# Scores over 128 rows filled up with zeros, a mask moved from VectorE to GpSimd, and a new order, in a gated mix of linear attention and softmax attention

## The chip, the cores and the metric

The kernel runs on one core of a Trainium2 chip. The metric is the device time of one execution in microseconds (us), the median of several runs; lower is better.

## The reference

The input x has 2048 rows of 1024 columns. Two attention blocks read it, each with 32 heads of 32 columns, and a gate mixes their outputs. All data is 32-bit.

```
g = sigmoid((x * gate_w).sum(-1))
# block A: linear attention
q, k, v = split(x @ A_wqkv);  phi(t) = where(t > 0, t + 1, exp(t)) + 1e-6
kv  = phi(k).T @ v            # per head, 32 x 32
z   = phi(k).sum(over rows)   # per head
a   = (phi(q) @ kv) / (phi(q) . z + 1e-6) @ A_wo
# block B: softmax attention
b   = softmax(q @ k.T * 32 ** -0.5) @ v @ B_wo      # per head, q, k, v of x @ B_wqkv
out = g * a + (1 - g) * b
```

## The kernel before

Products that need more precision than one pass gives are made of three: each operand is split into a high and a low part, and `three` (L150 to L152) accumulates high x high, high x low and low x high in one PSUM bank, each pass 128 rows by 512 columns.

The work runs in stages. First half of V of block B, then all of Q and K (parts kept in DRAM as `qk_d`), on TensorE alone. Then four streams are interleaved by a planner. `maxima` makes scores of one head and takes the row maxima on VectorE (L695, L700); it runs one head and 12 passes (`LEAD`) ahead of the next stream. `heads_` makes the same scores transposed, one head later, with the negative maxima added by the product itself, and ScalarE takes the exponential (L831, L835); a pair of passes is one of each, 64 for every head. After every four tiles of 128 keys the products P V follow as a block of 32 matmuls on 32 columns each (L922), and the sums of P are kept by GpSimd (L877, L881, three quarters) and VectorE (L890). `linear` is the linear block in units of one row tile and one chunk of columns, 24 passes each: the second half of V ("v"), keys and values ("kv", four chunks), queries ("q", two chunks) and output ("o", two chunks). `output` is the last projection.

A head's scores need three products as well, of 32 rows each; they are stacked into one: `load_head` (L665 to L675) puts high, high, low parts of Q and high, low, high parts of K into rows 0 to 95 of two big tiles. Three pairs of such tiles rotate, a head's parts being loaded two heads ahead on SP's queue. Rows 96 and 97 of K hold ones, written by GpSimd when a tile is first used, and rows 96 and 97 of Q the high and low part of the negative maxima, which two DMAs bring (L720) once the head's maxima are done. So the maxima's scores go over 96 rows (L695) and the transposed scores over 98 (L831).

For the keys, `keys` (from L492) sums v phi(k) of four heads at a time in a 128 x 128 block of `kvb`; only the 32 x 32 blocks on its diagonal belong to a head. When a chunk's last row tile is in, two VectorE products with `heads` (ones on those blocks, zeros elsewhere) clear the rest (L509). The blocks are next read by `split_w` for the output's weights (L456).

The order on each engine is written out by hand in advance: the planner keeps a modelled time for every engine, from costs in microseconds (`MM` a matmul, `AV` and `AV_SWITCH` a block of P V products and the change to it), and lets the stream go on whose start is due and which lags most behind its rate. The linear stream's rate is counted in passes per pair: `RATE_Q` while queries run (a unit counts as 26 there, with its transposes), and for keys and output what then remains.

Of the kernel before, what the change touches and what calls it, by code (L numbers as in the profile page):

```python
# [18 lines left out]
P = 128  # L19
DH = 32  # L20
C = 512
# [5 lines left out]
AV_STEP = 4  # L27
WO_SLOT = 4
RESERVE = 56.0
RATE_Q = 1.75  # L30
AHEAD = {"head": 0, "max": 6, "lin": 6, "out": 0}
MM = 0.232
AV, AV_SWITCH = 0.88, 0.3
LATENCY = {"pe": 0.225, "act": 0.39, "dve": 0.36, "pool": 0.2}
SLACK = 0.4
WARM = 8
# [7 lines left out]
def kernel(  # L44
# [19 lines left out]
    nc = tc.nc  # L64
# [12 lines left out]
    def f32(ap):  # L77
        return ap.bitcast(F32)
# [24 lines left out]
    heads = sb.tile([P, P], F32, name="heads")  # L103
# [3 lines left out]
    kvb = sb.tile([P, NK, P], F32, name="kvb")  # L107
# [15 lines left out]
    bank = [psum.tile([P, C], F32, name=f"bank{i}") for i in range(8)]  # L123
# [34 lines left out]
    def use(eng, cost, *after):  # L158

        T[eng] = max(T[eng], *after, 0.0) + cost  # L160
        return T[eng] + LATENCY[eng]
# [9 lines left out]
    def defer(fn, at, cost=0.6, rank=1, prev=None):  # L171
        item = Later(fn, at, cost, rank, prev)
        later.append(item)
        return item
# [16 lines left out]
    def need(items):  # L191

        for item in items:
            if item.end is None:
                run(item)

    def ended(items, *also):

        if any(item.end is None for item in items):
            return None  # L200
        return max([0.0, *also] + [item.end for item in items])

    def fill(until):

        while True:
            fit = [it for it in later if due(it) and max(T["dve"], it.at) + it.cost <= until]
            if not fit:
                return
            run(min(fit, key=lambda it: (it.at > T["dve"] + 0.1, it.rank)))
# [6 lines left out]
    def bank_at():  # L216

        times = [ended(readers[b], free[b]) for b in RING if not held[b]]
        return min((at for at in times if at is not None), default=None)

    def take():

        idle = [b for b in RING if not held[b]]
        times = {b: ended(readers[b], free[b]) for b in idle}
        b = min(idle, key=lambda b: (times[b] is None, times[b] or 0.0))
        need(readers[b])
        free[b] = ended(readers[b], free[b])
        readers[b].clear()
        held[b] = True
        return b  # L230

    def give(b, at=0.0, items=()):

        held[b] = False
        free[b] = max(free[b], at)
        readers[b].extend(items)

    def both(*times):

        return None if None in times else max(times)  # L240
# [192 lines left out]
    def lin_pe(cost, *after):  # L433
        lin_done[0] += cost
        return use("pe", cost * MM, *after)

# [53 lines left out]
    def keys(c, t, pk, va, todo):  # L490

        yield lambda: both(ended(todo), bank_at())  # L492
        need(todo)
        b = take()
        pb = bank[b]
        end = lin_pe(2.0, free[b])
        for g in range(HC // P):
            nc.tensor.matmul(pb[:, g * P:(g + 1) * P], va[:, g * P:(g + 1) * P], pk[:, g * P:(g + 1) * P],  # L498
                             start=True, stop=True)
        acc = kvb[:, c * (HC // P):(c + 1) * (HC // P), :].rearrange("p k c -> p (k c)")  # L500

        def total(_):
            if t == 0:
                nc.vector.tensor_copy(acc, pb[:, :HC])
            else:
                nc.vector.tensor_add(acc, pb[:, :HC], acc)
            if t == NT - 1:
                for g in range(c * (HC // P), (c + 1) * (HC // P)):
                    nc.vector.tensor_mul(kvb[:, g, :], kvb[:, g, :], heads)  # L509

        item = defer(total, end, 0.34 if t < NT - 1 else 1.0, 1, k_left[-1] if k_left else None)
        give(b, 0.0, [item])
        k_left.append(item)
# [142 lines left out]

    stack_ready = [None] * H
    rows_ready = [None] * H  # L660
    s_done, st_done = [0], [0]
# [3 lines left out]
    def load_head(h):  # L665
        g, r = divmod(h, 4)
        rows = slice(r * DH, (r + 1) * DH)
        q, k = stack[h % 3]
        if h < 3:
            nc.gpsimd.memset(f32(k[3 * DH:3 * DH + 2, :]), 1.0)  # L670
        for b, (qp, kp) in enumerate(((0, 0), (0, 1), (1, 0))):
            nc.sync.dma_start(f32(q[b * DH:(b + 1) * DH, :]), qk_d[0][qp][g][rows, :])
            nc.sync.dma_start(f32(k[b * DH:(b + 1) * DH, :]), qk_d[1][kp][g][rows, :])
        stack_ready[h] = T["pe"] + 10.0
# [8 lines left out]
    def maxima():  # L683

        for h in range(H):
            yield lambda: stack_ready[h]
            q, k = stack[h % 3]
            m = mx[h % 2]
            for i in range(NT * NJ):
                t, j = divmod(i, NJ)  # L690
                if i:
                    yield bank_at
                b = take()
                end = use("pe", MM, free[b])
                nc.tensor.matmul(bank[b], q[:3 * DH, t * P:(t + 1) * P], k[:3 * DH, j * C:(j + 1) * C],  # L695
                                 start=True, stop=True)
                s_done[0] += 1
                fill(end + LATE)
                give(b, use("dve", 0.605, end))
                nc.vector.tensor_reduce(m[:, t, j:j + 1], bank[b], AX.X, ALU.max)  # L700
            rows(h, q, mneg[h % 2])
# [103 lines left out]
    def heads_():  # L805
        pr_t.extend(big_tile(6 + i, F32) for i in range(NPR))
        lacc_t.extend(big_tile(i, F32) for i in LACC)
        spare = big_tile(SPARE, F32)
        raws[2:6] = [spare[:, i * C:(i + 1) * C] for i in range(4)]
        o_ring.append(spare)  # L810
        o_ring.extend(pr_t[((H - 1) * NT + t) % NPR] for t in (NT - 6, NT - 4, NT - 3, NT - 2, NT - 1))
        tail = None
        for h in range(H):
            q, k = stack[h % 3]
            last = h == H - 1
            av_, sums = attend(h, lacc_t[h % 2])
            for t in range(NT):
                i = (h * NT + t) % NPR
                for j in range(NJ):
                    if j:  # L820
                        yield bank_at
                    elif t:
                        yield lambda: both(ended(pr_left[i], pr_free[i]), bank_at())
                    else:
                        yield lambda: both(ended(pr_left[i], pr_free[i]), bank_at(), rows_ready[h])
                    if j == 0:
                        need(pr_left[i])
                        pr_left[i].clear()
                    b = take()
                    end = use("pe", MM, free[b], rows_ready[h])  # L830
                    nc.tensor.matmul(bank[b], k[:3 * DH + 2, t * P:(t + 1) * P],  # L831
                                     q[:3 * DH + 2, j * C:(j + 1) * C], start=True, stop=True)
                    end = use("act", 0.49, end, pr_free[i])
                    give(b, end)
                    nc.scalar.activation(pr_t[i][:, j * C:(j + 1) * C], bank[b], AF.Exp, scale=SCALE)  # L835
                    st_done[0] += 1
                    if j == 1 and t and t % AV_STEP == 0:
                        yield from av_(t - AV_STEP)
                    elif j == 1 and tail:
                        yield from tail(NT - AV_STEP)  # L840
                        tail = None
                    if j == 2 and t == 0 and h + 2 < H:
                        load_head(h + 2)
                        load_v(h + 2)
                pr_end[i] = end
                sums(t)
                if last and t >= WO_SLOT:
                    wo_load()
                    if t >= WO_SLOT + 2:
                        wo_split()  # L850
                    else:
                        wo_load()
            tail = av_
        yield from tail(NT - AV_STEP)
        for items in pr_left:
            need(items)
        over["head"] = True
        load_all()
# [115 lines left out]
    def out_pe(n, c, k):  # L974
# [5 lines left out]
        for _ in three(bank[b], stat, [wo_part(k, p)[:, sl] for p in range(2)], k):  # L980
            use("pe", MM, free[b])

# [57 lines left out]
    steps = H * NT * NJ  # L1040
    rates = {"q": RATE_Q, "v": 0.0}
    rates["kv"] = rates["o"] = (cost["kv"] + cost["o"] - RESERVE) / (steps - cost["q"] / RATE_Q)
    goal = [warm]
# [107 lines left out]
```

## Time and profile before

| | before |
|---|---|
| median of 3 runs | 2994.87 us (2991.62 to 2995.91) |
| the profiled execution | 2999.18 us |
| its span, first to last instruction | 2997.4 us |
| mean granted TensorE clock | 0.997 |
| busy: TensorE, VectorE, GpSimd, ScalarE | 99%, 70%, 57%, 51% |

The profile is of one execution. PE is TensorE's matmuls, PEld its weight loads, DVE is VectorE, ACT ScalarE, POOL GpSimd and SP the engine that issues the DMAs. L695 is line 695 of the kernel. A matmul's length on the timeline is longer than the distance to the next one's start, since matmuls are pipelined: what one costs in a dense run is the distance of starts. Shapes such as 96*128 are rows by columns of the weights.

### The profile page before, as it was taken

Reading aid. Unit: us, or ns where it says so; the run is one execution under the profiler, and the core shown is the slowest. Engines: PE = TensorE matmul, PEld = TensorE weight load, DVE = VectorE, ACT = ScalarE, POOL = GpSimd, SP = SyncE. Lnnn points to the kernel's source line nnn. Section 1 sums busy time; section 2 is a strip of 40 time slices with the busy share of each in tenths; the row PEclk is TensorE's granted clock in tenths of the full one; section 3 lists DMA queues with packets and bytes.
Section 4 is the critical chain, followed back from the end, with each engine's and each line's share of the span. In section 5 each row is a group of like instructions: output and inputs, shape, how many; then the busy total and the mean of one; then the engine's idle time right before and its main releaser. Section 6 shows DMA issues by size and latency. Waiting matters only on the chain.

```text
span 2997.4 us, 41699 instructions
## 1 busy us (share of the span) xinstructions
PE 2975.5 (99%) x15072; PEld 2105.9 (70%) x15072; DVE 2109.7 (70%) x3464; ACT 1527.6 (51%) x2840; POOL 1721.8 (57%) x578
## 2 busy tenths in 40 slices
PE   9999999999999999999999999999999999999999
PEld 8888888766666666666666666666665666666687
DVE  3222115878888888878888889999998888886322
ACT  4111110566666656656666666666665655656200
POOL 0000000578887879878978886786676777773000
PEclk9999999999999999999999999999999999999999
DMA  6787333433434333333333344454442543424542
GB/s 192 216 265 224 120 114 92 124 85 89 117 88 99 90 98 99 96 82 110 95 85 85 108 119 118 121 152 128 117 122 100 126 117 100 112 84 142 204 158 70
DMA packets 259871, 364.51 MB, mean 122 GB/s; under 512 B 86480, under 2 KB 163280, under 8 KB 253520
## 3 DMA queue, kind: packets, MB, share of 16 engines
q1 hardware_dynamic: 259664, 361.84, 41.6%
q8 instruction: 119, 1.95, 0.3%
q14 instruction: 88, 0.72, 0.1%
HBM read 260.57 MB, written 100.66 MB: 121 GB/s over the span
## 4 chain that ended last, share of the span: by engine, by line
PE 93%; DVE 5%; DMA 1%; ACT 1%; issue 0%; SPq 0%; POOL 0%; ACTq 0%; DVEq 0%
PE bank L831 16%; PE bank L150 15%; PE bank L152 15%; PE bank L695 15%; PE bank L151 15%; PE bank L922 14%; DVE mx L700 2%; PE bank L498 1%; PE bank L739 1%; DVE bank L746 1%; DVE bank L890 0%; PE bank L456 0%; DMA big<-oA 0%; DVE kvb L509 0%; PE bank L535 0%
## 5 line engine op out<-in xcount | busy, mean ns | idle before, releaser
L881 POOL TENSOR_TENSOR big<-big,big 128x1536 f32<-128x1536 f32 x434 | 1516.3, 3494 | 305.5 <-ACT big L835 285.3
L700 DVE TENSOR_REDUCE mx<-bank 128x1 f32<-128x512 f32 x2048 | 1319.7, 682 | 321.1 <-PE bank L695 313.9
L835 ACT ACTIVATE big<-bank 128x512 f32<-128x512 f32 x2048 | 1184.1, 599 | 683.7 <-PE bank L831 639.0
L695 PE MATMUL bank<-big,big 96*128 96x512 f32 x2048 | 830.1, 406 | 5.1 <-DVE mx L700 2.1
L831 PE MATMUL bank<-big,big 98*128 98x512 f32 x2048 | 826.9, 404 | 2.6 <-DVE mx L700 2.4
L150 PE MATMUL bank<-big,big 128*128 128x512 f32 x2048 | 807.7, 394 | 6.8 <-DMA big<-oA 3.6
L152 PE MATMUL bank<-big,big 128*128 128x512 f32 x2048 | 805.6, 393 | 1.2 <-DMA big<-oA 0.8
L151 PE MATMUL bank<-big,big 128*128 128x512 f32 x2048 | 805.6, 393 | 0.0
L831 PEld LDWEIGHTS bank<-big,big 98*128 98x128 f32 x2048 | 389.6, 190 | 182.4 <-issue 80.2
L695 PEld LDWEIGHTS bank<-big,big 96*128 96x128 f32 x2048 | 388.0, 189 | 121.3 <-issue 14.7
L922 PE MATMUL bank<-big,mid 128*32 128x512 f32 x4096 | 465.2, 594 | 0.0
L150 PEld LDWEIGHTS bank<-big,big 128*128 128x128 f32 x2048 | 387.9, 189 | 95.4 <-DMA big<-oA 4.0
L152 PEld LDWEIGHTS bank<-big,big 128*128 128x128 f32 x2048 | 388.0, 189 | 85.9 <-DMA big<-oA 1.7
L151 PEld LDWEIGHTS bank<-big,big 128*128 128x128 f32 x2048 | 388.0, 189 | 83.1 <-issue 0.8
L922 PEld LDWEIGHTS bank<-big,mid 128*32 128x32 f32 x4096 | 123.1, 110 | 284.7 <-issue 284.7
L670 POOL MEMSET big<- 2x2048 f32 x3 | 5.4, 1806 | 544.4 <-PE bank L151 463.0
L890 DVE TENSOR_TENSOR bank<-bank,big 128x512 f32<-128x512 f32 x434 | 300.0, 691 | 14.4 <-ACT big L835 11.7
L257 DVE TENSOR_TENSOR mid<-bank,mid 128x512 fp32r<-128x512 f32 x64 | 44.3, 692 | 264.6 <-ACT mid L256 264.6
L256 ACT CAST mid<-bank 128x512 fp32r<-128x512 f32 x64 | 37.6, 587 | 291.6 <-PE bank L152 277.0
L877 POOL TENSOR_TENSOR big<-big,big 128x1536 f32<-128x1536 f32 x31 | 108.6, 3502 | 133.9 <-ACT big L835 128.1
L746 DVE RECIPROCAL bank<-bank 128x128 f32<-128x128 f32 x128 | 123.5, 965 | 5.8 <-PE bank L739 2.6
L257 DVE TENSOR_TENSOR big<-mid,big 128x512 fp32r<-128x512 f32 x96 | 64.1, 687 | 71.0 <-ACT big L256 70.9
(75 smaller groups left out, 1055.8 us busy)
## 6 DMA issues: line engine op xcount, KB each, us to landing
big<-xs SPq DMA_DIRECT2D x192, 512.0 KB, 4.1
big<-qk SPq DMA_DIRECT2D x192, 256.0 KB, 6.5
qk<-mid SPq DMA_DIRECT2D x128, 256.0 KB, 2.8
big<-oA SPq DMA_DIRECT2D x64, 512.0 KB, 4.8
xs<-big SPq DMA_DIRECT2D x64, 256.0 KB, 4.2
oA<-mid SPq DMA_DIRECT2D x64, 256.0 KB, 2.3
mid<-in_b_wqkv SPq DMA_DIRECT2D x48, 256.0 KB, 3.8
mid<-in_xT SPq DMA_DIRECT2D x32, 256.0 KB, 4.1
```

Source lines behind the costliest of these rows:

```text
L150: yield nc.tensor.matmul(ps, sh, mh_, start=(kt == 0), stop=False)
L151: yield nc.tensor.matmul(ps, sh, ml_, start=False, stop=False)
L152: yield nc.tensor.matmul(ps, sl, mh_, start=False, stop=(kt == NK - 1))
L695: nc.tensor.matmul(bank[b], q[:3 * DH, t * P:(t + 1) * P], k[:3 * DH, j * C:(j + 1) * C], start=True, stop=True)
L700: nc.vector.tensor_reduce(m[:, t, j:j + 1], bank[b], AX.X, ALU.max)
L746: nc.vector.reciprocal(pl[:, sl], pl[:, sl])
L831: nc.tensor.matmul(bank[b], k[:3 * DH + 2, t * P:(t + 1) * P], q[:3 * DH + 2, j * C:(j + 1) * C], start=True, stop=True)
L835: nc.scalar.activation(pr_t[i][:, j * C:(j + 1) * C], bank[b], AF.Exp, scale=SCALE)
L877: nc.gpsimd.tensor_add(lacc[:, :QP], pr(0)[:, :QP], pr(1)[:, :QP])
L881: nc.gpsimd.tensor_add(lacc[:, :QP], lacc[:, :QP], pr(t)[:, :QP])
L890: nc.vector.tensor_add(lacc[:, QP:] if t == NT - 1 else l_b[:, :n], l_b[:, :n], src)
L922: nc.tensor.matmul(av_b[j * DH:(j + 1) * DH, :], v[:, t, :], pr(t)[:, j * C:(j + 1) * C], start=(t == 0), stop=(t == NT - 1))
```

## The change

Scores' products, both ways round, go over all 128 rows. GpSimd fills rows 96 to 127 of both tiles with zeros at a tile's first use (the ones in K's rows 96 and 97 come after that). From the fourth head on, when a tile of Q is used again, a DMA copies two rows of zeros (98 and 99) over rows 96 and 97, in which the maxima of an earlier head stand. The mask on `kvb` goes from VectorE to GpSimd. Four planner constants change: `RATE_Q`, `MM`, `AV`, `AV_SWITCH`.

```diff
-RATE_Q = 1.75
+RATE_Q = 2.0
-MM = 0.232
-AV, AV_SWITCH = 0.88, 0.3
+MM = 0.2275
+AV, AV_SWITCH = 0.865, 0.35
...
             if t == NT - 1:
                 for g in range(c * (HC // P), (c + 1) * (HC // P)):
-                    nc.vector.tensor_mul(kvb[:, g, :], kvb[:, g, :], heads)
+                    nc.gpsimd.tensor_mul(kvb[:, g, :], kvb[:, g, :], heads)
...
         q, k = stack[h % 3]
         if h < 3:
+            for part in (q, k):
+                nc.gpsimd.memset(f32(part[3 * DH:, :]), 0.0)
             nc.gpsimd.memset(f32(k[3 * DH:3 * DH + 2, :]), 1.0)
+        else:
+            nc.sync.dma_start(f32(q[3 * DH:3 * DH + 2, :]), f32(q[3 * DH + 2:3 * DH + 4, :]))
...
-                nc.tensor.matmul(bank[b], q[:3 * DH, t * P:(t + 1) * P], k[:3 * DH, j * C:(j + 1) * C],
+                nc.tensor.matmul(bank[b], q[:, t * P:(t + 1) * P], k[:, j * C:(j + 1) * C],
                                  start=True, stop=True)
...
-                    nc.tensor.matmul(bank[b], k[:3 * DH + 2, t * P:(t + 1) * P],
-                                     q[:3 * DH + 2, j * C:(j + 1) * C], start=True, stop=True)
+                    nc.tensor.matmul(bank[b], k[:, t * P:(t + 1) * P], q[:, j * C:(j + 1) * C],
+                                     start=True, stop=True)
```

## Rows read from the trace of the kernel before

**Rows 1.** Page, part 1: busy us of each engine (share of the span), instructions.

```profile
PE 2975.5 (99%) x15072; PEld 2105.9 (70%) x15072; DVE 2109.7 (70%) x3464; ACT 1527.6 (51%) x2840; POOL 1721.8 (57%) x578
```

**Rows 2.** Groups by line, 475.4 to 2778.1, TensorE: shapes, count, busy us, mean ns.

```profile
L831 PE MATMUL bank<-big,big 98*128 98x512 f32 x2048 | 826.9, 404 | 2.6 <-DVE mx L700 2.4
L922 PE MATMUL bank<-big,mid 128*32 128x512 f32 x4064 | 461.6, 594 | 0.0
L150 PE MATMUL bank<-big,big 128*128 128x512 f32 x1065 | 423.6, 398 | 1.5 <-DVE mx L700 0.7 <-DVE mid L749 0.5
```

**Rows 3.** Timeline of TensorE during projections: start us, length us, line, shapes.

```profile
329.67 0.39 PE L150 MATMUL bank<-big,big 128*128 128x512 f32 x1
...
333.98 0.39 PE L151 MATMUL bank<-big,big 128*128 128x512 f32 x1
```

**Rows 4.** Timeline of TensorE at the end of the last head.

```profile
2770.42 0.39 PE L151 MATMUL bank<-big,big 128*128 128x512 f32 x1
...
2778.12 0.40 PE L150 MATMUL bank<-big,big 128*128 128x512 f32 x1
...
2790.13 0.39 PE L152 MATMUL bank<-big,big 128*128 128x512 f32 x1
...
2794.67 0.39 PE L151 MATMUL bank<-big,big 128*128 128x512 f32 x1
```

**Rows 5.** Timeline of TensorE while V's second half meets the first maxima.

```profile
498.02 0.40 PE L695 MATMUL bank<-big,big 96*128 96x512 f32 x1
...
502.92 0.40 PE L150 MATMUL bank<-big,big 128*128 128x512 f32 x1
```

**Rows 6.** Windows: us, then busy PE, PEld, DVE, ACT, POOL; clock, DMA, GB/s.

```profile
498.00:503.00 5.00, 5.00 (x23) 4.05 (x22) 3.78 (x7) 0.59 (x1) 0.00 (x0) 1.00 0.14 52
...
2790.00:2795.00 5.00, 5.00 (x23) 3.85 (x21) 4.49 (x8) 1.18 (x3) 0.00 (x0) 1.00 0.84 278
```

**Rows 7.** Timeline of all engines at the end of the first chunk of keys.

```profile
852.06 3.56 DVE L509 TENSOR_TENSOR kvb<-kvb,heads 128x128 f32<-128x128 f32 x2
...
853.50 0.40 PE L695 MATMUL bank<-big,big 96*128 96x512 f32 x1
...
856.28 0.80 PE L831 MATMUL bank<-big,big 98*128 98x512 f32 x1 [2.38 <-DVE mx L700]
...
861.99 0.63 PE L695 MATMUL bank<-big,big 96*128 96x512 f32 x1
```

**Rows 8.** Windows, just behind the hole of rows 7.

```profile
856.90:862.00 5.10, 5.10 (x14) 3.95 (x12) 3.63 (x7) 1.99 (x4) 5.02 (x2) 0.50 0.04 7
```

**Rows 9.** Groups by line, whole run: the mask, and GpSimd's sum of phi(k).

```profile
L612 POOL TENSOR_TENSOR mid<-mid,mid 128x256 f32<-128x256 f32 x60 | 44.0, 733 | 23.3 <-DVE mid L607 23.2
...
L509 DVE TENSOR_TENSOR kvb<-kvb,heads 128x128 f32<-128x128 f32 x8 | 10.4, 1342 | 0.1
```

**Rows 10.** Windows: within the query stage, and within the output stage.

```profile
1760.00:2260.00 500.00, 496.12 (x2623) 330.60 (x2619) 458.29 (x762) 320.46 (x599) 362.86 (x109) 1.00 0.45 128
...
2320.00:2560.00 240.00, 240.00 (x1279) 161.39 (x1275) 197.12 (x311) 141.04 (x246) 182.86 (x53) 1.00 0.45 117
```

**Rows 11.** Groups by line, TensorE: two rows of 1760:2260, then two of 2320:2560.

```profile
L695 PE MATMUL bank<-big,big 96*128 96x512 f32 x433 | 175.8, 408 | 2.5 <-DVE mx L700 0.9 <-ACT big L835 0.6 <-DVE mid L749 0.5
...
L150 PE MATMUL bank<-big,big 128*128 128x512 f32 x235 | 94.0, 400 | 1.1 <-DVE mid L749 0.5 <-DVE mx L700 0.5
...
L695 PE MATMUL bank<-big,big 96*128 96x512 f32 x224 | 88.9, 397 | 0.0
...
L151 PE MATMUL bank<-big,big 128*128 128x512 f32 x111 | 43.9, 395 | 0.0
```

**Rows 12.** Groups by line, GpSimd, whole run: busy us, mean ns, idle before.

```profile
L881 POOL TENSOR_TENSOR big<-big,big 128x1536 f32<-128x1536 f32 x434 | 1516.3, 3494 | 305.5 <-ACT big L835 285.3
...
L670 POOL MEMSET big<- 2x2048 f32 x3 | 5.4, 1806 | 544.4 <-PE bank L151 463.0 <-PE bank L152 81.4
```

**Rows 13.** DMA issues: count, KB each, median us from issue to landing.

```profile
big<-mh SPq DMA_DIRECT2D x32, 8.0 KB, 1.8
```

## The prediction

> **What bounds the kernel now.** I read the busy shares first [rows 1]: TensorE is busy for 2975.5 of the 2997.4 us, every other engine for 70% or less. A busy share says little of a pipelined engine, so the next question is how fast one matmul follows the next, and there the timelines differ by stretch. While V, Q and K are projected, all matmuls have 128 rows, and 20 of them start between 329.67 and 333.98: 4.31 / 19 = 0.2268 us each [rows 3]. During attention the linear work (128 rows) is interleaved with scores' passes of 96 or 98 rows. Between 2770.42 and 2778.12 34 matmuls start, one row after the other without a hole: 7.70 / 33 = 0.2333 us each [rows 4]. Once the last 98-row pass is past, 21 matmuls of 128 rows start from 2790.13 to 2794.67: 4.54 / 20 = 0.2270 us [rows 4]. So TensorE loses 6.6 ns on each matmul wherever row counts are mixed, those of 128 rows included.
>
> Is it the mixture, or what else goes on in attention? From 498.02 to 502.92 22 matmuls start, only 6 of them with 96 rows: 4.90 / 21 = 0.2333 us again [rows 5]. The price doesn't grow with the share of short passes. GpSimd does nothing in that stretch, and VectorE is busy for 3.78 of 5 us [rows 6]; in the stretch at full pace VectorE is busy for 4.49 of 5 us [rows 6]. So neither of these two engines' traffic sets the 0.2333. The likeliest reading is that consecutive matmuls use different numbers of rows; what each scores' pass has besides, an accumulation and a signal of its own, is the first rival below.
>
> **The change part by part.**
> *128 rows.* From the first scores' pass to the last (475.4 to 2778.1) there are 2048 + 2048 short matmuls (L831 stands in the rows, L695 has the same count) and 3 x 1065 of the linear work (L150 stands there, L151 and L152 have the same count) [rows 2]: 7291. All have 128 rows afterwards. Bounds: nothing gained (0) to 7291 x 0.0066 = 48 us; a loss is excluded by rows 3, since 128-row passes of the same width and type never start later than 0.227 apart when nothing is waited for. I take the rate of rows 3, less the first matmuls after each block of P V products: there are 4064 / 32 = 127 such blocks [rows 2], each ends the steady run, and I give the five matmuls behind each no gain: (7291 - 635) x 0.0066 = 43.9 us.
> What speaks against it is a rule of the Trainium skill: "TensorE: Matmul & The Clock Gate", section "Why this matters for your kernels", has a single matmul of K = 32 take the same time as one of K = 128, and its section "Back-to-back issue gap" has a spacing that depends on columns alone. By that rule the term is 0. The trace agrees with it for runs of one row count and disagrees for mixtures, 0.2333 against 0.2268 at the same 512 columns.
>
> *Mask on GpSimd.* Eight VectorE products of kvb by heads go, 10.4 us in all, 1342 ns each [rows 9]. At the first chunk's end two of them hold VectorE from 852.06 for 3.56 us; the maxima behind them come late, banks run out, and TensorE starts nothing between 853.50 and 856.28 [rows 7]. After this hole its granted clock is 0.50, the lower level, 1.2 GHz [rows 8]. From 853.50 to 861.99 there are 14 steps: 8.49 - 14 x 0.2333 = 5.2 us lost [rows 7]. The other three chunk ends hold no such hole; I give them 1 us together. Gain 6 us, bounds 0 and 5.2 + (10.4 - 3.56) = 12. On GpSimd the nearest row is its 128x256 sum, 733 ns [rows 9], so 8 x 0.37 = 3 us, behind at most one 3.5 us addition, which holds nothing up: the masked sums are read only by the output weights' products, a whole stage of queries later.
>
> *Zeros.* Six memsets of 32 rows for the first three heads, by the nearest row 1.81 us each (2 rows, as long) [rows 12], up to 2048 / 1536 x 3.49 = 4.7 us by an addition's row [rows 12]: 11 to 28 us of GpSimd. Four of them come while GpSimd stands still (its idle time before these memsets is 544.4 us [rows 12]); the last two delay its first sum by 3.6 to 9.4 us, hidden by the six buffers of P. From the fourth head on, one more DMA of two rows, 29 in all. A row of the maxima lands in 1.8 us [rows 13]; the head's first maxima come 64 - 12 = 52 pairs of passes later, 52 x 1.07 = 56 us (pair from rows 11). Behind it in SP's queue stand the head's own six loads, with the same cover, and a transfer for the linear work, which is issued a unit ahead (24 matmuls, over 5 us). I cost it at 0, up to 2 us if the cover were gone.
>
> *Order.* The planner's times change, and the query stage gets 2.0 instead of 1.75 linear passes per scores' pass: a unit of 26 every 13 pairs instead of 14.9. Total work is unchanged; the question is whether VectorE then binds. Before, 433 pairs took 500 us, 1.155 each, with VectorE busy 458.29 / 433 = 1.058 (92%) [rows 10, 11]. In the output stage it is 197.12 / 224 = 0.880 per pair [rows 10, 11]; the difference times 14.9 is 2.65 us per unit. Afterwards: 0.880 + 2.65 / 13 = 1.084. TensorE before: 2 + 3 x 235 / 433 = 3.63 matmuls x 0.2333 = 0.847, the rest of the pair 0.308 [rows 10, 11]; afterwards (2 + 24 / 13) x 0.2268 + 0.308 = 1.180. 92% again, so TensorE still leads. I take 0, with 10 us to either side, since every wait may move, and a hole like that of [rows 7] costs clock as well [rows 8].
>
> **Sum.** 43.9 + 6 = 50 us off the profiled execution's 2999.2 us (span 2997.4): 2949. The median of the runs is 4.3 us below that execution: 2945.
>
> **The rivals.**
> *The rows don't matter.* The 0.2333 could come from the accumulation that every scores' pass opens and the signal that it sends, which stay. For: every short pass has both. Against: in rows 5 the pace is the same with six in 22 as in rows 4. Then only the mask gains: 2989. Chance 0.09. The rule of the Trainium skill's "TensorE: Matmul & The Clock Gate" named above leads here too.
> *Half is eaten in the query stage.* There the pair holds 0.308 us beside matmuls, in the output stage 240 / 224 - (2 + 3 x 111 / 224) x 0.2333 = 0.258 [rows 10, 11]: 0.05 are already lost to VectorE's bursts. Denser units could double that: 416 x 0.05 = 21 us, so 2966. For: VectorE's share of 92%. Against: by the sum above the share doesn't rise. Chance 0.11.
> *Slower: holes that halve the clock.* A burst of VectorE's that holds up the maxima as in [rows 7] stops TensorE and lowers its clock, 5.2 us each [rows 7, 8]. With a unit's chain every 13 pairs and 32 units this can come often; beyond nine such holes (50 / 5.2) the gain is gone, and with one in every third unit, eleven or twelve, it is 2945 + 60 = 3005. For: VectorE is in order, and the maxima wait behind the chain. Against: 32 such chains before left almost none of these. Chance 0.06.
>
> **How the numbers follow.** The forecast has 0.74, with 2930 to 2962 as its own range (the term of 128 rows from 36 to 48, the mask 0 to 12, the order 10). Up to 2975 it takes in most of the second rival; below 2930 nothing is known that leads there. About 0.2% (6 us) can be told from no change. Faster by more: the forecast, the second rival and some of the first, 0.88; within: 0.05; slower: 0.07.
>
> **What would show it.** Right: in the mixed stretches consecutive starts 0.227 apart, for scores' passes and linear ones alike; no hole at the first chunk's end, and the mask on GpSimd at under 1 us each; VectorE near 92% in the query stage. Wrong: starts still 0.233 apart (first rival), runs of starts 0.6 us apart in the query stage (second), more stretches with the clock at 0.50 (third).

## The result and the profile after

The changed kernel takes 2942.7 us (median of 4 runs, 2940.84 to 2943.51), the kernel before 2995.35 (4 runs): a ratio of 0.9826, interval 0.9809 to 0.9843, 52.7 us less. The forecast was 2945. The profiled execution took 2942.07 us, its span is 2940.0.

Two parts of the page of the kernel after: busy us of each engine, and the shares of the chain that ended last.

```profile
PE 2926.5 (100%) x15072; PEld 2085.9 (71%) x15072; DVE 2088.9 (71%) x3456; ACT 1528.7 (52%) x2840; POOL 1737.9 (59%) x592
...
PE 98%; DVE 1%; DMA 1%; ACT 0%; issue 0%; SPq 0%; DVEq 0%; ACTq 0%
```

And the chain of the kernel before:

```profile
PE 93%; DVE 5%; DMA 1%; ACT 1%; issue 0%; SPq 0%; POOL 0%; ACTq 0%; DVEq 0%
```

TensorE was busy for 99% of the span and is now for 100%, which says little; the chain says more. VectorE set the pace for 5% of the span before and for 1% now: some of the gain is not a faster matmul but fewer places where TensorE waits for VectorE.

What answers to [rows 5] and [rows 4], the timeline of TensorE (start us, length us, line, shapes) where maxima meet the linear work, and where the last scores' passes do:

```profile
498.07 0.39 PE L150 MATMUL bank<-big,big 128*128 128x512 f32 x1
...
502.83 0.39 PE L700 MATMUL bank<-big,big 128*128 128x512 f32 x1
```

```profile
2716.14 0.39 PE L836 MATMUL bank<-big,big 128*128 128x512 f32 x1
...
2721.80 0.39 PE L151 MATMUL bank<-big,big 128*128 128x512 f32 x1
```

In the first 22 matmuls start, 4.76 / 21 = 0.2267 us apart; in the second 26, 5.66 / 25 = 0.2264. Both were 0.2333 before. Passes of the same work, in the same places, with the same banks, accumulations and signals, run at the full pace once all have 128 rows.

The mask, the memsets, and GpSimd's sum by line (busy us, mean ns, idle before), which answer to [rows 9] and [rows 12]:

```profile
L612 POOL TENSOR_TENSOR mid<-mid,mid 128x256 f32<-128x256 f32 x60 | 44.3, 738 | 17.6 <-DVE mid L607 17.4
...
L672 POOL MEMSET big<- 32x2048 f32 x6 | 10.8, 1807 | 533.0 <-PE bank L151 460.5 <-DVE big L466 71.5 <-PE bank L152 0.9
...
L509 POOL TENSOR_TENSOR kvb<-kvb,heads 128x128 f32<-128x128 f32 x8 | 3.5, 469 | 0.0
```

A product of the mask takes GpSimd 469 ns, where 370 were taken for it, and VectorE had taken 1342 on average. A memset of 32 rows takes what one of 2 rows took, 1.81 us. Where the first mask comes, the timeline of GpSimd has it between two additions:

```profile
853.17 7.12 POOL L886 TENSOR_TENSOR big<-big,big 128x1536 f32<-128x1536 f32 x2
860.25 0.88 POOL L509 TENSOR_TENSOR kvb<-kvb,heads 128x128 f32<-128x128 f32 x2
861.08 10.62 POOL L886 TENSOR_TENSOR big<-big,big 128x1536 f32<-128x1536 f32 x3
```

TensorE has no hole there any more: 13 matmuls start in this stretch, 2.76 / 12 = 0.230 us apart.

```profile
859.66 0.39 PE L151 MATMUL bank<-big,big 128*128 128x512 f32 x1
...
862.42 0.39 PE L700 MATMUL bank<-big,big 128*128 128x512 f32 x1
```

Within the query stage, the windows (us; busy PE, PEld, DVE, ACT, POOL; clock, DMA, GB/s), which answer to [rows 10]:

```profile
1770.00:2200.00 430.00, 428.59 (x2298) 293.20 (x2291) 399.32 (x667) 279.99 (x524) 311.31 (x95) 1.00 0.45 133
```

VectorE is busy for 399.32 of 430 us, 93%, where 92% was the forecast; before it was 92% as well.

### The profile page after: what moved, and what is told of

Read it like the earlier page. It is cut to its first block, busy times and chain, and to the rows that moved or that the text cites. A ratio compares the mean times of both kernels' runs of the same rounds, so it can differ in the third digit from the quotient of the medians.

```text
span 2940.0 us, 41729 instructions
## 1 busy us (share of the span) xinstructions
PE 2926.5 (100%) x15072; PEld 2085.9 (71%) x15072; DVE 2088.9 (71%) x3456; ACT 1528.7 (52%) x2840; POOL 1737.9 (59%) x592
## 4 chain that ended last, share of the span: by engine, by line
PE 98%; DVE 1%; DMA 1%; ACT 0%; issue 0%; SPq 0%; DVEq 0%; ACTq 0%
PE bank L836 16%; PE bank L700 16%; PE bank L150 16%; PE bank L152 16%; PE bank L151 16%; PE bank L927 15%; PE bank L744 1%; PE bank L498 1%; DVE mx L705 1%; PE bank L456 0%; PE bank L535 0%; DMA mid<-in_xT 0%; DVE bank L895 0%; DMA big<-oB 0%; DMA big<-oA 0%; DVE bank L751 0%
## 5 line engine op out<-in xcount | busy, mean ns | idle before, releaser
L705 DVE TENSOR_REDUCE mx<-bank 128x1 f32<-128x512 f32 x2048 | 1314.4, 682 | 306.4 <-PE bank L700 303.0
L700 PE MATMUL bank<-big,big 128*128 128x512 f32 x2048 | 816.7, 399 | 1.4 <-ACT mid L315 0.9
L836 PE MATMUL bank<-big,big 128*128 128x512 f32 x2048 | 817.3, 399 | 0.0
L150 PE MATMUL bank<-big,big 128*128 128x512 f32 x2048 | 801.9, 392 | 6.5 <-DMA big<-oA 3.0
L152 PE MATMUL bank<-big,big 128*128 128x512 f32 x2048 | 799.8, 391 | 0.6 <-DVE big L257 0.4
L151 PE MATMUL bank<-big,big 128*128 128x512 f32 x2048 | 799.4, 390 | 0.0
L836 PEld LDWEIGHTS bank<-big,big 128*128 128x128 f32 x2048 | 384.5, 188 | 173.6 <-issue 70.1
L700 PEld LDWEIGHTS bank<-big,big 128*128 128x128 f32 x2048 | 384.7, 188 | 109.0 <-issue 19.6
L150 PEld LDWEIGHTS bank<-big,big 128*128 128x128 f32 x2048 | 385.2, 188 | 90.7 <-DVE mx L705 3.4
L152 PEld LDWEIGHTS bank<-big,big 128*128 128x128 f32 x2048 | 385.1, 188 | 83.0 <-DVE big L257 1.7
L151 PEld LDWEIGHTS bank<-big,big 128*128 128x128 f32 x2048 | 385.2, 188 | 79.1 <-issue 0.8
L672 POOL MEMSET big<- 32x2048 f32 x6 | 10.8, 1807 | 533.0 <-PE bank L151 460.5
```

The source lines that it names most:

```text
L150: yield nc.tensor.matmul(ps, sh, mh_, start=(kt == 0), stop=False)
L151: yield nc.tensor.matmul(ps, sh, ml_, start=False, stop=False)
L152: yield nc.tensor.matmul(ps, sl, mh_, start=False, stop=(kt == NK - 1))
L700: nc.tensor.matmul(bank[b], q[:, t * P:(t + 1) * P], k[:, j * C:(j + 1) * C], start=True, stop=True)
L836: nc.tensor.matmul(bank[b], k[:, t * P:(t + 1) * P], q[:, j * C:(j + 1) * C], start=True, stop=True)
```

## The experiments

Each kernel's edit is against the kernel before or the changed one, as it says. The runs are from several chips; the kernel before, run beside each, had medians of 2994.7 to 2997.0, so that kernels of different chips are best compared by their ratios to it (0.001 is 3 us).

**One part at a time.** 128 rows alone: the zeros, the copy and the four row slices of the change, nothing else of it. The slices:

```diff
-nc.tensor.matmul(bank[b], q[:3 * DH, t * P:(t + 1) * P], k[:3 * DH, j * C:(j + 1) * C],
+nc.tensor.matmul(bank[b], q[:, t * P:(t + 1) * P], k[:, j * C:(j + 1) * C],
...
-nc.tensor.matmul(bank[b], k[:3 * DH + 2, t * P:(t + 1) * P],
-                 q[:3 * DH + 2, j * C:(j + 1) * C], start=True, stop=True)
+nc.tensor.matmul(bank[b], k[:, t * P:(t + 1) * P],
+                 q[:, j * C:(j + 1) * C], start=True, stop=True)
```

> The kernel before with one part of the change: scores' products over 128 rows with zeros; mask on VectorE, order by the old constants. Theory (mixed row counts cost 6.6 ns on each of 7291 matmuls): starts 0.227 apart in the mixed stretches, 2995 - 44 = 2951 us, 2947 to 2958. Rival (order or mask carried the gain): 2985 or more.

Measured: 2962.1 us, ratio 0.9889 (0.9875 to 0.9902), against 2995.9: 33.9 us. The rival is out, and so is the size: 2951 was expected. The timeline of this kernel at the first chunk's end has the mask's hole still in it:

```profile
845.51 0.39 PE L699 MATMUL bank<-big,big 128*128 128x512 f32 x1
848.02 0.62 PE L835 MATMUL bank<-big,big 128*128 128x512 f32 x1 [2.11 <-DVE mx L704]
...
850.99 0.63 PE L835 MATMUL bank<-big,big 128*128 128x512 f32 x1
...
852.46 0.39 PE L152 MATMUL bank<-big,big 128*128 128x512 f32 x1
852.68 0.40 PE L699 MATMUL bank<-big,big 128*128 128x512 f32 x1
```

Nothing starts for 2.51 us, the next eight matmuls start 2.97 / 7 = 0.42 apart, and by 852.46 they are back at 0.22. Faster passes do not take a hole away.

The mask alone:

```diff
-nc.vector.tensor_mul(kvb[:, g, :], kvb[:, g, :], heads)
+nc.gpsimd.tensor_mul(kvb[:, g, :], kvb[:, g, :], heads)
```

> The kernel before with only the mask moved to GpSimd. Theory (the hole at the first chunk's end and its slow clock cost 5.2 us, the other chunk ends 1 us together): 2989 us, no hole at 853. Rival (the hole is filled by another wait a little later): 2995, no difference.

Measured: 2991.1 us, ratio 0.9986 (0.9977 to 0.9994): 4.9 us, where 6 were expected. The hole at 853 is gone: 17 matmuls start from 851.75 to 855.49, 3.74 / 16 = 0.234 us apart.

The order alone:

```diff
-RATE_Q = 1.75
-MM = 0.232
-AV, AV_SWITCH = 0.88, 0.3
+RATE_Q = 2.0
+MM = 0.2275
+AV, AV_SWITCH = 0.865, 0.35
```

> The kernel before with only the four planner constants. Theory (total work is unchanged and the order gives nothing by itself): 2995 us, 10 to either side. Rival (the order carries part of the gain): under 2980. Rival (units closer together make holes on TensorE): over 3005.

Measured: 2980.9 us, ratio 0.9954 (0.9942 to 0.9967): 15.0 us. This falls between the theory and the first rival: the order is worth something by itself, though its modelled 0.2275 for a matmul is not what this kernel's mixed passes take. Part of the 15.0 may be clock: with VectorE still making the mask, TensorE starts nothing for 2.09 us from 860.92, but in this trace the granted clock stays at 1.00 behind that hole, where it fell to 0.50 in [rows 8]. The three parts alone make 33.9 + 4.9 + 15.0 = 53.8 us, together 52.7: within the noise they add up.

**Each part taken back.** The changed kernel with the four old constants:

```diff
-RATE_Q = 2.0
-MM = 0.2275
-AV, AV_SWITCH = 0.865, 0.35
+RATE_Q = 1.75
+MM = 0.232
+AV, AV_SWITCH = 0.88, 0.3
```

> The changed kernel with the four planner constants of the kernel before (so 128 rows and the mask on GpSimd). Theory (the order gives nothing): 2943 us, within 3. Rival (what is over the 44 us of the rows and the 5 of the mask comes from the order, above all queries at 2.0): 2950 or more.

Measured: 2957.5 us, ratio 0.9876 (0.9859 to 0.9892): the rival, and the order is worth 14.8 us here too (15.0 by the ratios).

The changed kernel with the mask on VectorE:

```diff
-nc.gpsimd.tensor_mul(kvb[:, g, :], kvb[:, g, :], heads)
+nc.vector.tensor_mul(kvb[:, g, :], kvb[:, g, :], heads)
```

> The changed kernel with the mask on VectorE again. Theory (mask worth 6 us by the hole that it makes): 2949 us, with a hole of over 2 us on TensorE at a chunk's end and the clock at 0.50 behind it. Rival (in the new order the maxima aren't due when the mask comes): 2943, no such hole.

Measured: 2950.6 us, ratio 0.9851 (0.9836 to 0.9865): 7.9 us more than the changed kernel. The two longest holes at chunk ends, on the timeline of TensorE at the first and the third, and the windows behind them (the last column but two is the granted clock):

```profile
857.10 0.39 PE L700 MATMUL bank<-big,big 128*128 128x512 f32 x1
859.62 0.50 PE L836 MATMUL bank<-big,big 128*128 128x512 f32 x1 [2.13 <-DVE mx L705]
859.96 0.40 PE L151 MATMUL bank<-big,big 128*128 128x512 f32 x1
```

```profile
1459.30 0.39 PE L700 MATMUL bank<-big,big 128*128 128x512 f32 x1
1461.47 0.50 PE L836 MATMUL bank<-big,big 128*128 128x512 f32 x1 [1.78 <-DVE mx L705]
...
1463.24 0.63 PE L152 MATMUL bank<-big,big 128*128 128x512 f32 x1
1463.67 0.63 PE L700 MATMUL bank<-big,big 128*128 128x512 f32 x1
```

```profile
860.00:865.00 5.00, 4.86 (x22) 3.60 (x21) 5.00 (x10) 3.88 (x9) 4.92 (x2) 1.00 0.39 140
1461.60:1465.00 3.40, 3.40 (x10) 2.67 (x11) 3.40 (x6) 1.44 (x3) 3.32 (x2) 0.57 0.00 0
```

The mechanism is the one of [rows 7]: TensorE waits for the maxima behind the mask (2.13 and 1.78 us by the rows). The clock was forecast to fall behind such a hole, and it fell to 0.57 behind the second, where matmuls start 0.43 apart, but stayed at 1.00 behind the first, which is the longer one.

Not all of the 7.9 us is the mask's. Before any mask this trace has another hole, 2.33 us from start to start, ended by ScalarE, with the lower clock behind it:

```profile
547.92 0.39 PE L151 MATMUL bank<-big,big 128*128 128x512 f32 x1
550.25 0.50 PE L700 MATMUL bank<-big,big 128*128 128x512 f32 x1 [1.94 <-ACT mid L315]
```

```profile
550.30:553.00 2.70, 2.70 (x7) 2.09 (x8) 2.50 (x5) 1.62 (x4) 0.00 (x0) 0.58 0.79 228
```

The changed kernel has 1.32 us there and keeps its clock. From the first scores' pass to the first product of the keys this trace takes 100.4 us and the changed kernel's 97.8, so 2.6 us of the difference come from there.

Why the mask holds VectorE for so long is seen in the kernel before, where its first product meets an addition of GpSimd's:

```profile
851.81 3.46 POOL L881 TENSOR_TENSOR big<-big,big 128x1536 f32<-128x1536 f32 x1
...
852.06 3.36 DVE L509 TENSOR_TENSOR kvb<-kvb,heads 128x128 f32<-128x128 f32 x1
```

The addition ends at 855.27 and the product at 855.42. The four traces with the mask on VectorE (before, 128 rows alone, order alone, and this one) have 32 of these products: 14 take 0.28 us, and the other 18, of 0.71 to 4.05 us, each end 0.15 to 0.16 us after a GpSimd instruction that was running when they began. So the time of [rows 7] is a wait for GpSimd, not work of VectorE's.

**Is it the count, the share or the change?** The changed kernel with all split products over 98 rows, both scores' products and the three linear passes; the linear passes leave the last 30 rows of each 128 of their contraction out:

```diff
-yield nc.tensor.matmul(ps, sh, mh_, start=(kt == 0), stop=False)
+yield nc.tensor.matmul(ps, sh[:98], mh_[:98], start=(kt == 0), stop=False)
...
-nc.tensor.matmul(bank[b], q[:, t * P:(t + 1) * P], k[:, j * C:(j + 1) * C],
+nc.tensor.matmul(bank[b], q[:98, t * P:(t + 1) * P], k[:98, j * C:(j + 1) * C],
...
```

> The changed kernel with every split product over 98 rows: scores and maxima read 98 of their 128 rows, and the linear passes leave rows 98 to 127 of their contraction out. Theory (a change of the row count between consecutive matmuls costs, the count itself nothing): starts 0.227 apart, 2943 us, 5 to either side. Rival (a short pass is slow, and slows its neighbours): 0.2333 in all 10240 of them, 2943 + 10240 x 0.0066 = 3010 us.

Measured: 2944.2 us, ratio 0.9829 (0.9814 to 0.9844), the changed kernel's time. Its timeline in the stretch of [rows 5]:

```profile
498.04 0.39 PE L700 MATMUL bank<-big,big 98*128 98x512 f32 x1
...
503.03 0.39 PE L151 MATMUL bank<-big,big 98*128 98x512 f32 x1
```

23 starts, 4.99 / 22 = 0.2268 us apart. A pass over 98 rows is as fast as one over 128, as long as its neighbours have 98 too.

The changed kernel with 127 of 128 rows for maxima and scores:

```diff
-nc.tensor.matmul(bank[b], q[:, t * P:(t + 1) * P], k[:, j * C:(j + 1) * C],
+nc.tensor.matmul(bank[b], q[:127, t * P:(t + 1) * P], k[:127, j * C:(j + 1) * C],
...
-nc.tensor.matmul(bank[b], k[:, t * P:(t + 1) * P], q[:, j * C:(j + 1) * C],
+nc.tensor.matmul(bank[b], k[:127, t * P:(t + 1) * P], q[:127, j * C:(j + 1) * C],
```

> The changed kernel with maxima and scores over 127 of the 128 rows (the last holds zeros), the linear passes over 128. Theory (any difference in the row count costs): 0.2333, 2987 us. Rival (only a difference of a group of rows counts, or of many): 0.227, 2943 us.

Measured: 2974.9 us, ratio 0.9933 (0.9918 to 0.9947): 32.2 us more than the changed kernel. The same stretch:

```profile
497.85 0.40 PE L700 MATMUL bank<-big,big 127*128 127x512 f32 x1
...
502.98 0.40 PE L150 MATMUL bank<-big,big 128*128 128x512 f32 x1
```

23 starts, 5.13 / 22 = 0.2332. One row less, and the whole price of the 96 is back. The size expected, 44 us, was too large again; the pace expected was right.

The changed kernel with 96 rows for the maxima alone:

```diff
-nc.tensor.matmul(bank[b], q[:, t * P:(t + 1) * P], k[:, j * C:(j + 1) * C],
+nc.tensor.matmul(bank[b], q[:3 * DH, t * P:(t + 1) * P], k[:3 * DH, j * C:(j + 1) * C],
```

> The changed kernel with the maxima's passes over 96 rows again, the transposed scores over 128. Theory (mixture costs every matmul in the stretch, whatever the share of short ones): 0.2333 on nearly all of some 7200, 2943 + 44 = 2987 us. Rival (each short pass costs its own 13 ns, and half of them are left): 2943 + 24 = 2967 us.

Measured: 2972.9 us, ratio 0.9927 (0.9912 to 0.9942): 30.2 us more than the changed kernel. By the totals alone this lies between the two expectations. The timeline decides, in the middle of the keys, with one pass in three or so of 96 rows:

```profile
1406.54 0.40 PE L150 MATMUL bank<-big,big 128*128 128x512 f32 x1
...
1409.81 0.40 PE L700 MATMUL bank<-big,big 96*128 96x512 f32 x1
```

15 starts, 3.27 / 14 = 0.2336. They come close behind a block of the keys' products, which lengthens distances by itself (next section), so the whole trace is the better witness. Between the first and the last scores' pass, and among consecutive passes of 512 columns that start 0.2 to 0.245 us apart, two neighbours that both have 128 rows are 0.2333 apart on average here (3068 pairs) and 0.2281 in the changed kernel: every matmul pays, not each short pass 13 ns. And half the short passes cost 30.2 us where all of them, at 127 rows, cost 32.2.

**Which of the constants?** The changed kernel with the old rate, and with two higher ones:

```diff
-RATE_Q = 2.0
+RATE_Q = 1.75
```

> The changed kernel with queries at 1.75 passes again, the other three constants new. By the runs so far the order is worth 15 us, from fewer holes on TensorE in the query stage and behind it. Theory (the modelled times of a matmul and a block are what thins the holes): 2943 to 2946 us. Rival (the rate does it): 2953 to 2957, with 7 us of holes in the query stage as under the old constants.

Measured: 2962.2 us, ratio 0.9881 (0.9865 to 0.9898). The theory falls: without the rate nothing of the order's gain is left, and the time lies above even the rival's 2953 to 2957. The kernel with all four old constants had 0.9876, which can't be told from this one.

```diff
-RATE_Q = 2.0
+RATE_Q = 2.25
```

> The changed kernel with queries at 2.25 passes. If the rate thins the holes, a little more of it keeps them thin: 2938 to 2945 us. If VectorE binds from here on, its busy share within the query stage passes 95% and holes of 0.35 us and more return: over 2950.

Measured: 2949.8 us, ratio 0.9840 (0.9825 to 0.9855). It lies between the two expectations, 7 us above the changed kernel (4 by the ratios, whose intervals overlap). VectorE's share within the query stage (1770 to 2200) is 387.08 of 430 us, 90%, so it does not bind by the sign that was set for it. What the trace does have is one hole of 3.10 us from 1987.11 that the changed kernel lacks, with the clock at 0.50 for 3.4 us behind it; it ends when ScalarE, which waited for a transfer of weights, goes on (timeline of both engines):

```profile
1989.04 0.62 ACT L464 CAST big<-mid 128x512 fp32r<-128x512 f32 x1 [3.14 <-DMA mid<-in_a_wqkv]
...
1990.21 0.79 PE L836 MATMUL bank<-big,big 128*128 128x512 f32 x1 [2.71 <-ACT big L840]
```

```diff
-RATE_Q = 2.0
+RATE_Q = 2.5
```

> The changed kernel with queries at 2.5 passes. VectorE needs 0.880 + 2.65 / 10.4 = 1.135 us for a pair, TensorE (2 + 24 / 10.4) x 0.2268 + 0.26 = 1.24: the share stays at 92%. If holes follow the share: 2943, within 5. If bursts count more the closer the units are: over 2950.

Measured: 2949.6 us, ratio 0.9843 (0.9828 to 0.9858), the same as at 2.25, again between the two expectations. No rate here beats 2.0.

Last, the new rate with the old modelled times:

```diff
-MM = 0.2275
-AV, AV_SWITCH = 0.865, 0.35
+MM = 0.232
+AV, AV_SWITCH = 0.88, 0.3
```

> The changed kernel with only the rate of the queries new (2.0), a matmul and a block of P V products modelled by the old times. With the runs at 1.75 (old times 2957, new times 2962) and the changed kernel (2.0, new times, 2943) it closes a square. Theory (the rate alone thins the holes, the modelled times do nothing): 2938 to 2945 us. Rival (it takes both): 2950 or more.

Measured: 2950.1 us, ratio 0.9854 (0.9838 to 0.9871): by a hair the rival. By the ratios the rate saves 6.6 us with the old times (0.9876 to 0.9854), where the intervals overlap, and 16.5 with the new (0.9881 to 0.9826), where they don't; the new times do nothing at 1.75 and save 8.4 at 2.0, where the intervals still touch. So the order's gain needs the new rate. How much the rate brings by itself, and how much the new times add, is not clear of the noise.

Where the time goes is seen in the chain of waits over the query stage and the start of the next, by line. The first is the kernel before, then the new rate with old times, then the changed kernel, then the changed kernel at 1.75:

```profile
by line: PE bank L831 16.4%; PE bank L695 16.1%; PE bank L922 15.8%; DVE mx L700 10.1%; PE bank L150 8.0%; PE bank L152 7.7%; PE bank L151 7.6%; DVE bank L746 3.5%; DVE bank L890 2.0%; issue 1.7%; PE bank L535 1.5%; DVE bank L624 1.1%; DVE 
```

```profile
by line: PE bank L927 15.9%; PE bank L836 15.6%; PE bank L700 15.5%; PE bank L150 9.3%; DVE mx L705 9.2%; PE bank L151 9.0%; PE bank L152 9.0%; DVE bank L751 2.8%; DVE bank L895 2.1%; PE bank L535 2.0%; PE bank L456 1.4%; issue 1.4%; DVE mi
```

```profile
by line: PE bank L836 18.6%; PE bank L700 18.4%; PE bank L927 18.0%; PE bank L150 10.7%; PE bank L152 10.4%; PE bank L151 10.4%; DVE mx L705 3.6%; PE bank L535 2.4%; PE bank L456 1.5%; PE bank L744 1.2%; DVE bank L895 0.8%; DVE bank L751 0.
```

```profile
by line: PE bank L927 15.9%; DVE mx L705 15.0%; PE bank L836 14.8%; PE bank L700 13.6%; PE bank L150 7.2%; PE bank L152 6.8%; PE bank L151 6.8%; DVE bank L751 3.2%; DVE bank L895 2.9%; issue 2.3%; PE bank L535 1.8%; DVE bank L624 1.2%; DVE 
```

The maxima's reductions on VectorE (L700, and L705 afterwards) hold 10.1% of the chain before, then 9.2%, 3.6% and 15.0%. Among the three kernels with 128 rows the order of these shares is that of the times. A share of the chain is not lost time, since TensorE works beside it; it tells how often VectorE led. Lost time can be counted as well: the distances of 0.245 us and more between neighbouring passes of 512 columns, from the first scores' pass to the last (waits, steps at the lower clock, and the first steps behind other shapes), hold over 0.2267 us each 64.3 us in the kernel before and 50.4 with the order alone. With 128 rows and the mask on GpSimd it is 66.3 us at 1.75 with the new times, 58.2 with the old constants, 51.8 at the new rate with the old times, and 48.8 in the changed kernel. So the order takes away waits of TensorE's and slow steps behind them.

## Why the prediction came out right, step by step

The total was 50 us by forecast and is 52.7; two of its terms were off, in opposite directions. That they nearly cancel is luck.

*What bounds it, and why.* Right. The loss comes with different row counts in one stretch: it is gone with 128 everywhere and with 98 everywhere, and back with 127 beside 128. It isn't tied to the change itself, since in the kernel before two neighbours of 128 rows start 0.2337 us apart on average too (1165 pairs). The first rival, the accumulation and signal of a scores' pass, is out, since they are all still there. The rule of the Trainium skill's "TensorE: Matmul & The Clock Gate" (section "Back-to-back issue gap") that spacing depends on columns alone holds in the steady runs of each kernel of one row count, 0.2268 us for 98 rows and 0.2267 for 128, and fails in the mixture.

*128 rows: 43.9 us forecast, 33.9 measured alone.* The pace of a long run was right, and so was the number of matmuls, but they gain less on average than the 6.6 ns. I gave none of the gain to five matmuls behind each block of P V products and all of it to the rest. Products of other shapes also end a steady run, and the pace comes back by degrees. On the timeline of the changed kernel, behind four products of 128 columns for the keys:

```profile
703.85 0.61 PE L498 MATMUL bank<-mid,mid 128*128 128x128 f32 x4
...
704.52 0.39 PE L836 MATMUL bank<-big,big 128*128 128x512 f32 x1
...
706.61 0.39 PE L700 MATMUL bank<-big,big 128*128 128x512 f32 x1
706.83 0.39 PE L836 MATMUL bank<-big,big 128*128 128x512 f32 x1
...
708.87 0.39 PE L700 MATMUL bank<-big,big 128*128 128x512 f32 x1
```

From 704.52 to 706.61 10 matmuls start, 2.09 / 9 = 0.232 apart; from 706.83 to 708.87 10, 2.04 / 9 = 0.2267. This place is one of the slow ones: over the whole trace the third start behind another shape is 0.2330 on average, the sixth 0.2293, the ninth 0.2279. So the sentence that 128-row passes never start later than 0.227 apart holds in long runs alone. Of all starts of the trace between the first and the last scores' pass that follow a 512-column pass by 0.2 to 0.245 us, what they hold over 0.2267 each adds up to 46.2 us before (6630 starts) and 9.5 us after (6642): 36.7 us gained in the pace, 5.5 ns each. The run of this part alone has the same 9.5 us, and its longer distances hold what they did before (64.9 us, 64.3). Its trace is 36.5 us shorter than the one of the kernel before (spans of 2960.9 and 2997.4); the medians differ by only 33.9 because the traced execution of the kernel before, 2999.18 us, lay above the median.

*Mask: 6 us forecast, 4.9 measured alone, 7.9 in the new order.* Right, by the hole that it makes, though 2.6 of the 7.9 us arise before the first mask. The 3.56 us of VectorE were read as the products' own time; they are a wait for GpSimd's addition. On GpSimd the products take their turn between additions, and no hole follows.

*Zeros: nothing.* Nothing shows them: the memsets take 10.8 us of GpSimd, and the pace in [rows 5]'s stretch is full from the first maxima on. They were not measured by themselves.

*Order: 0 with 10 to either side, 15.0 measured alone and 14.8 beside the other parts.* This step failed: the size was outside its own bounds. I argued from VectorE's share, which the new rate leaves at 92%; the share did stay (93%), and the time changed. By the chain of waits, what counts within the stage is how often a unit's chain of operations and the other bursts on VectorE hold up the maxima, which hold the banks that TensorE needs, and an average share doesn't tell that. What went of waits and slow steps was counted (64.3 us to 50.4, and 58.2 to 48.8); that VectorE's bursts are what ended them is read from the chain, not tested. The second rival, holes that grow with denser units, had the sign wrong at 2.0. At 2.25 and 2.5 some of the gain may be lost again, too little to be sure of, and the one long hole at 2.25 is a wait for a transfer. Why 2.0 has the fewest such places was not settled: what was shown is that the gain needs the rate, not how its units come to lie beside the other bursts.

*The third rival*, holes that halve the clock, did not come: the changed kernel's mean granted clock is 0.999, where it was 0.997.

So the forecast met the total with one term 10 us too large (7 by the traces) and another 15 us too small.

## What to carry to other kernels

Where matmuls of different numbers of rows follow each other, compare the distance of starts in mixed stretches with that in stretches of one kind; if it differs, filling operands up to one common row count cost no time on TensorE here and gave back 2.8% of each dense mixed stretch (0.2333 to 0.2268). The full count isn't needed, the same count is. A change in a hand-made order is to be measured, not argued from busy shares: at the same share of VectorE the order was worth 15 us. And the long time of an operation on one engine can be a wait for another: a mean of 1342 ns was made of 0.28 us products and of waits of up to 3.4 us.

## What the runs showed of the hardware that was not expected

A single row is enough: 127 beside 128 rows gives 0.2332 us, 128 beside 128 gives 0.2267. The price is paid by all matmuls of a mixed stretch, about 6.5 ns each, whether six in 22 are short or one in three, and two neighbours of 128 rows pay it too. After products of another shape, such as the keys' of 128 columns, the pace comes back over about ten passes (0.2330 us at the third start, 0.2279 at the ninth, on average in the changed kernel). VectorE's product of `kvb` and `heads` takes 0.28 us, but where an instruction of GpSimd's was already running it ended 0.15 us after that one, up to 4.05 us from its start. And the length of a hole does not tell whether the clock falls: in one execution the granted clock fell behind holes of TensorE of 2.33 and 2.17 us from start to start and not behind one of 2.52 (0.58, 0.57 and 1.00 in the windows behind them).
